# Batch 2's transposes issued earlier, both transposes of a pair ahead of their copies, score and value bursts merged

## The chip, the cores and the metric

The kernel runs on one core of one Trainium2 chip. The metric is the device time of one execution in microseconds (us); of several executions the median is given. The core's engines are TensorE (PE, matmuls), VectorE (DVE), ScalarE (ACT), GpSimd (POOL) and SyncE (SP). Each works through its own instructions in the order in which they stand; semaphores make one engine wait for another or for a DMA. SP and POOL also issue the DMAs.

## The reference

Eight batches, eight heads, 576 tokens, head dimension 64: attention in a window of 32 tokens to each side, with 8 global tokens that see all and are seen by all, and behind it a gated feed-forward layer on the 4608 tokens.

```python
scores = scale * np.matmul(q, k.transpose(0, 1, 3, 2))
mask = np.abs(pos[:, None] - pos[None, :]) <= window
mask = mask | is_global[:, None] | is_global[None, :]
scores = np.where(mask, scores, -1000000000.0)
...
attn = attn / (np.sum(attn, axis=-1, keepdims=True) + 1e-09)
attn_out = np.matmul(attn, v)
x = attn_out.transpose(0, 2, 1, 3).reshape(B * S, H * D)
silu = g * (1.0 / (1.0 + np.exp(-g)))        # g = x @ w_gate
out = silu * (x @ w_val) @ w_out
```

## The kernel before, in words

The feed-forward layer is the backbone. `ffn` (L647) works on 9 chunks of 512 tokens, and each chunk has 16 units: 12 gates and 4 outputs. A gate (`gate`, L650) makes 128 columns of both projections, pg and pv, with four matmuls each into two PSUM tiles of the pool `pf` (four buffers); ACT makes a tanh of pg (L663), DVE two products (gv L665, h L669). An output (`outp`, L673) makes 128 tokens of the result with 12 matmuls, ACT scales it to osb (L681, three buffers), and SP stores it (L683). The units are numbered through, and the number is called a slot.

The attention of a batch is cut into steps, which are put into gaps behind the units, so that PE has dense work around them:

- `step_T` (batches 0 and 1): PE transposes k and q of a pair of heads into PSUM; ACT copies kT (L346), DVE copies qT (L351). From batch 2 on kT and qT come by DMA: `cast_qk` (L105) has POOL write k and q as bf16 to DRAM (kf, qf), and `transpose_qk` (L113) has SP issue two transposing DMAs (L115, L119).
- `step_GT` transposes the gathered global keys and queries to gT; `step_S2` (L389) and `step_SG` (L371) are the scores of the global tokens, each a burst of 8 matmuls, an exponential on ACT and a mask product on DVE (p2, pg).
- `step_P2T` transposes p2, `step_AV2` (L420) makes the global tokens' values, and three DVE steps turn them into gvt.
- `step_S(u)`, u from 0 to 4 (L450): scores in the window, 16 matmuls, exponential (L458), band product on DVE (pt, L463).
- `step_AV(tp)`, tp from 0 to 3, and `step_AV8`: values from pg, gvt, pt, va and vb (L494, L503), then a normalisation on DVE (a reduction, a reciprocal, a product xa, L475 to L481). va is v by tokens in blocks of 128; vb is the same shifted by half a block, made from va by two DMAs that SP issues (`load_vb`, L123).
- `step_X(tp)` and `step_X8`: xa is transposed to xT, the feed-forward layer's input: by PE and a copy on ACT (L541, L547) for batches 0 to 2, by a DMA that SP issues for batches 3 to 7 (from XB = 3).

PSUM has three pools: `pf` with four buffers of one bank, `psc` and `pm` with one buffer of two banks each. Window scores, S2 and SG go to `psc`, most others to `pm`.

Batch 0 runs ahead of the first unit (the head). Batch 1 lies in the gaps of slots 0 to 17, one or two steps each; batch 2 starts at slot 19 with one gap a slot, and the later batches follow with a step every 1.08 or 1.1 slots (`STEP`, L55). `later` (L574) in batch b issues the transposes of batch b + 2, the gather of its global tokens and the cast of batch b + 3; `later_v` loads its v. Batch 1's `later` stands in gap 15 and asks for batch 3; the transposes of batch 2 are put at the front of gap 16:

```python
gaps[8].append(lambda: kqms.__setitem__(2, gather_mask(*gather(2))))
gaps[10].append(lambda: cast_qk(3))
for i, g in enumerate(last):
    gaps[16 + i] = g
gaps[16].insert(0, lambda: transpose_qk(2))
```

## Time and profile before

| | us |
|---|---|
| three executions | 394.91, 395.31, 396.77 |
| median | 395.31 |
| the profiled execution | 395.97 |
| its span, first to last instruction | 394.3 |
| PE busy in the span | 357.5 (91%) |
| DVE busy | 236.7 (60%) |
| ACT busy | 148.4 (38%) |
| POOL busy | 99.0 (25%) |
| mean granted clock of PE, of 1 | 0.961 |

The profile is of one execution. Its page gives the busy time of each engine, the same in 40 equal slices, the granted clock of PE, the chain of work that ended last, and groups of instructions with count, busy time, mean duration and the idle time ahead of them. Other views are the waits (who waited for whom), the timeline of an engine, windows (busy times in given stretches) and the chain of waits in order of time. A busy PE is not a PE at its peak, as matmuls are pipelined.

### The profile page before, as it was taken

The page shows a single profiled execution, that of the slowest core. Times are in us where ns is not written, and L with a number is a line of the kernel's source. Part 1 is how long each engine was busy: PE and PEld are TensorE (multiplying, and loading weights), DVE is VectorE, ACT ScalarE, POOL GpSimd, SP SyncE. Part 2 cuts the span into 40 slices and gives each one's busy share as a digit, 9 for nine tenths or more (in the row PEclk, how much of TensorE's full clock was granted, in tenths as well). Part 3 has the DMA queues.
Part 4 walks back from the last instruction along what each step waited for, and adds up shares of the span by engine and source line. Part 5 has one row for each costly group of instructions (what it writes and reads, how often), then busy time and mean ns, then how long its engine had stood idle before and what let it go on. Part 6 is the DMA issues. An engine that isn't in the chain of part 4 may idle for free.

```text
span 394.3 us, 7717 instructions
## 1 busy us (share of the span) xinstructions
PE 357.5 (91%) x3159; PEld 170.7 (43%) x3159; DVE 236.7 (60%) x467; ACT 148.4 (38%) x228; POOL 99.0 (25%) x114
## 2 busy tenths in 40 slices
PE   2458889992799999999999999999999999999995
PEld 2344444540254544444444444444444444444442
DVE  5645678352275388638963895489448935743750
ACT  2523445340253345234533533354235423323321
POOL 8836661746051143114412201100000000000000
PEclk9958999997589999999999999999999999999999
DMA  8999999999999799999989728952260121002002
GB/s 116 113 207 204 186 204 129 132 218 160 177 73 129 137 163 129 87 154 187 126 93 229 111 25 82 205 111 16 80 130 18 28 80 62 0 27 82 0 26 81
DMA packets 151987, 44.51 MB, mean 113 GB/s; under 512 B 138384, under 2 KB 146064, under 8 KB 151952
## 3 DMA queue, kind: packets, MB, share of 16 engines
q0 software_dynamic: 101472, 19.40, 59.9%
q1 hardware_dynamic: 50480, 24.63, 28.9%
q8 instruction: 24, 0.39, 0.4%
q14 instruction: 11, 0.09, 0.1%
HBM read 38.28 MB, written 16.52 MB: 139 GB/s over the span
## 4 chain that ended last, share of the span: by engine, by line
PE 82%; DMA 8%; DVE 3%; SPq 2%; ACT 2%; POOL 2%; issue 1%; DVEq 0%; POOLq 0%; ACTq 0%
PE pg L657 24%; PE po L676 24%; PE pv L657 22%; DMA qT<-qf 3%; PE ps_av L494 3%; PE ps_s L450 3%; PE ps_av L503 2%; DMA vb<-va 2%; DMA kg<-in_k_dram,gofs 1%; SPq L115 1%; DMA va<-in_v_dram 1%; PE ps_x L541 1%; PE ps_t L340 1%; PE ps_sg L371 1%; DVE h L669 1%
## 5 line engine op out<-in xcount | busy, mean ns | idle before, releaser
L657 PE MATMUL pg<-xT,wg_sb 128*128 128x512 bf16 x432 | 113.3, 385 | 1.4 <-ACT xT L547 1.4
L657 PE MATMUL pv<-xT,wv_sb 128*128 128x512 bf16 x432 | 112.6, 384 | 0.0
L663 ACT ACTIVATE th<-pg 128x512 bf16<-128x512 f32 x108 | 64.5, 597 | 92.2 <-PE pg L657 79.2
L665 DVE SCALAR_TENSOR_TENSOR gv<-th,pg 128x512 bf16<-128x512 bf16 x108 | 74.0, 685 | 41.8 <-ACT th L663 41.8
L676 PE MATMUL po<-wo_sb,h 128*128 128x512 bf16 x432 | 98.3, 380 | 0.0
L669 DVE TENSOR_TENSOR h<-gv,pv 128x512 bf16<-128x512 bf16 x108 | 74.3, 688 | 11.8 <-PE pv L657 0.8
L657 PEld LDWEIGHTS <-wv_sb 128*128 128x128 bf16 x432 | 42.7, 99 | 52.2 <-issue 2.2
L101 POOL DMA_DIRECT2D va<-in_v_dram x40 | 36.1, 1061 | 95.7 <-PE ps_av L503 82.1
L676 PEld LDWEIGHTS <-h 128*128 128x128 bf16 x432 | 40.1, 98 | 45.9
L657 PEld LDWEIGHTS <-wg_sb 128*128 128x128 bf16 x432 | 36.7, 98 | 41.8 <-issue 6.9
L681 ACT ACTIVATE osb<-po 128x512 f32<-128x512 f32 x36 | 21.5, 597 | 84.1 <-PE po L676 78.1
L463 DVE TENSOR_TENSOR pt<-pe,band 128x1024 bf16<-128x1024 bf16 (+1 forms) x40 | 25.6, 640 | 32.2 <-ACT pe L458 31.5
L458 ACT ACTIVATE pe<-ps_s 128x1024 bf16<-128x1024 f32 (+1 forms) x40 | 37.5, 939 | 17.0 <-PE ps_s L450 16.3
L475 DVE TENSOR_REDUCE den<-ps_av 128x8 f32<-128x16 f32 (+1 forms) x40 | 6.8, 170 | 35.7 <-PE ps_av L503 29.9
L481 DVE TENSOR_TENSOR xa<-ps_av,den 128x512 bf16<-128x512 f32 (+1 forms) x40 | 25.5, 638 | 1.6 <-DVE den L480 0.2
L494 PE MATMUL ps_av<-gvt,pg 128*64 128x264 bf16 x128 | 18.7, 303 | 2.1 <-DVE gvt L435 2.0
L503 PE MATMUL ps_av<-vb,pt 128*64 128x66 bf16 x256 | 18.3, 201 | 1.4 <-DMA vb<-va 1.4
L450 PE MATMUL ps_s<-qT,kT 64*128 64x64 bf16 x576 | 16.5, 197 | 3.0 <-ACT pe L458 1.6
L450 PEld LDWEIGHTS <-kT 64*128 64x128 bf16 x576 | 11.9, 98 | 17.0 <-issue 15.8
L503 PEld LDWEIGHTS <-pt 128*64 128x64 bf16 x512 | 18.3, 117 | 1.9 <-DMA vb<-va 1.7
L503 PE MATMUL ps_av<-va,pt 128*64 128x66 bf16 x256 | 18.5, 201 | 0.0
L108 POOL DMA_DIRECT2D qf<-in_q_dram x6 | 16.6, 2766 | 0.0
(92 smaller groups left out, 187.9 us busy)
## 6 DMA issues: line engine op xcount, KB each, us to landing
out_dram<-osb SPq DMA_DIRECT2D x36, 256.0 KB, 2.2
vb<-va SPq DMA_DIRECT2D x16, 264.0 KB, 7.6
kf<-in_k_dram POOLq DMA_DIRECT2D x6, 576.0 KB, 8.4
qf<-in_q_dram POOLq DMA_DIRECT2D x6, 576.0 KB, 14.0
va<-in_v_dram POOLq DMA_DIRECT2D x24, 128.0 KB, 3.9
va<-in_v_dram POOLq DMA_DIRECT2D x16, 96.0 KB, 12.7
wg_sb<-in_moe_w_gate_dram POOLq DMA_DIRECT2D x3, 512.0 KB, 10.4
wv_sb<-in_moe_w_val_dram POOLq DMA_DIRECT2D x3, 512.0 KB, 13.1
```

What stands on the lines that cost most here:

```text
L101: nc.gpsimd.dma_start(out=va[lo:hi, u, :, 0:D], in_=vs[t0 + lo : t0 + hi])
L450: nc.tensor.matmul(out=ps[:, par, 64 * slot : 64 * slot + 64], lhsT=kT[r : r + 64, hp, 64 * t : 64 * t + P], rhs=qTs[b][r : r + 64, hp, 64 ...
L458: nc.scalar.activation(out=pe, in_=ps[:, :, 0 : 64 * ns].rearrange("p r (s c) -> p r s c", c=64), func=AF.Exp, scale=SCALE,)
L463: nc.vector.tensor_tensor(out=pt.rearrange("p r s c -> p (r s) c"), in0=pe.rearrange("p r s c -> p (r s) c"), in1=bc(band, [[0, 2 * ns], [ ...
L481: nc.vector.tensor_tensor(out=xa.rearrange("p (g h) d -> p g h d", g=g), in0=bc(ps, pst + [[1, D]]), in1=bc(den, [[4, g], [1, 4], [0, D]]) ...
L494: nc.tensor.matmul(out=ps[64 * e : 64 * e + 64, hg], lhsT=st["pg"][:, P * tp + 64 * e : P * tp + 64 * e + 64], rhs=st["gv"].rearrange("p h ...
L503: nc.tensor.matmul(out=ps[64 * e : 64 * e + 64, hg, hl, :], lhsT=pt[:, hl % 2, 4 * (hl // 2) + 2 * (tp % 2) + e, :], rhs=(va if e == 0 els ...
L657: nc.tensor.matmul(out=ps[:, 0:n], lhsT=w[:, cc, P * fc : P * (fc + 1)], rhs=xT[:, cc, t0 : t0 + n], start=(cc == 0), stop=(cc == NCC - 1),)
L663: nc.scalar.activation(out=th[:, 0:n], in_=pg[:, 0:n], func=AF.Tanh, scale=0.5)
L665: nc.vector.scalar_tensor_tensor(out=gv[:, 0:n], in0=th[:, 0:n], scalar=1.0, in1=pg[:, 0:n], op0=ALU.add, op1=ALU.mult,)
L669: nc.vector.tensor_tensor(out=st["h"][:, fc, 0:n], in0=gv[:, 0:n], in1=pv[:, 0:n], op=ALU.mult)
L676: nc.tensor.matmul(out=po, lhsT=st["h"][:, fc, P * ts : P * (ts + 1)], rhs=wo_sb[:, fc, :], start=(fc == 0), stop=(fc == NFC - 1),)
```

## The change

- `load_vb` for batch 0 copies on DVE; the other batches keep the DMAs.
- `step_T` issues the 24 transposes of k and q, then both copies.
- `step_SG` uses `pm`; AV of batch 2 from tp = 1 on uses `psc`, and AV8 from batch 3 on.
- The head has GT ahead of the second table step, vb and P2T ahead of S(1), and AV2 ahead of S(3).
- S2 with SG, S(1) with AV2, S(3) with AV(0) and others share a gap. Batches 1 and 2 have the same list `mid`; batches 3 to 7 have 10 entries, 1.6 slots apart, in place of 14.
- The first two gates of chunk 0 are split by tokens: `first_gates` does 384 columns of both ahead of X(3) of batch 0 and 128 behind it. Units 0 and 1 are then empty, and batch 1's T steps start one slot later.
- The transposes of batch 2 move from the front of gap 16 to the end of gap 14.

```diff
@@ load_vb
+        if b == 0:
+            nc.vector.tensor_copy(out=vb[0:64], in_=va[64:128, 0:4])
+            nc.vector.tensor_copy(out=vb[64:128], in_=va[0:64, 1:5])
+            return vb
@@ step_T
-                if name == "k":
-                    nc.scalar.copy(
...
-                else:
-                    nc.vector.tensor_copy(
...
+            nc.scalar.copy(
+                out=kT[:, hp, WIN : WIN + S].rearrange("p (i j) -> p i j", j=LJ),
+                in_=pss[0].rearrange("p j i -> p i j"),
+            )
+            nc.vector.tensor_copy(
+                out=qTs[b][:, hp, :].rearrange("p (i j) -> p i j", j=LJ),
+                in_=pss[1].rearrange("p j i -> p i j"),
+            )
@@ step_SG
-            ps = psc.tile([P, 2, 512], FP32, tag="sc", name="ps_sg")
+            ps = pm.tile([P, 2, 512], FP32, tag="m", name="ps_sg")
@@ step_AV
-            pool, tag = (psc, "sc") if tp % 2 and b == 0 or tp and b == 1 else (pm, "m")
+            pool, tag = (psc, "sc") if tp % 2 and b == 0 or tp and b in (1, 2) else (pm, "m")
@@ step_AV8
+            if b >= XB:
+                full = psc.tile([P, 2, 512], FP32, tag="sc", name="ps_av8")
...
@@ step_X
+            if b == 0 and tp == 3:
+                ps = pm.tile([P, HP, P], BF16, tag="m", name="ps_x")
...
@@ the lists of steps
-                L(step_T, 2), L(step_T, 3), tables_b, L(step_GT), L(step_S2), L(step_SG),
-                L(step_S, 1), L(step_P2T), L(step_S, 3), vb, L(step_AV2),
+                L(step_T, 2), L(step_T, 3), L(step_GT), tables_b, L(step_S2), L(step_SG),
+                vb, L(step_P2T), L(step_S, 1), L(step_AV2), L(step_S, 3),
...
+        mid = [
+            [L(step_S2), L(step_SG)],
+            [L(step_P2T), L(step_S, 0)],
+            [L(step_S, 1), L(step_AV2)],
+            [L(step_S, 2)],
+            [L(step_S, 3), L(step_AV, 0)],
+            [L(step_X, 0), L(step_AV, 1)],
+            [L(step_X, 1), L(step_AV, 2)],
+            [L(step_X, 2), L(step_AV, 3)],
+            [L(step_X, 3), L(step_S, 4), later],
+        ]
+        end = [[L(step_AV8), later_v], [L(step_X8)]]
...
-                [L(step_GT)], [], [], [L(step_T, 0)], [L(step_T, 1)],
+                [L(step_GT)], [], [], [], [L(step_T, 0)], [L(step_T, 1)],
                 [L(step_T, 2), L(step_T, 3), vb],
...
+            ] + mid, end
         if b < XB:
...
+            return [[L(step_GT), vb]] + mid + end
         return [
             [L(step_GT), vb],
-            [L(step_S2)],
-            [L(step_SG)],
-            [L(step_P2T), L(step_S, 0)],
-            [L(step_S, 1)],
-            [L(step_AV2)],
+            [L(step_S2), L(step_SG)],
+            [L(step_S, 0), L(step_P2T)],
+            [],
+            [L(step_S, 1), L(step_AV2)],
             [L(step_S, 2)],
-            [L(step_AV, 0), L(step_X, 0)],
+            [L(step_S, 3), L(step_AV, 0), L(step_X, 0)],
             [L(step_AV, 1), L(step_X, 1)],
-            [L(step_S, 3)],
-            [L(step_AV, 2), L(step_X, 2)],
-            [L(step_S, 4), later],
-            [L(step_AV, 3), L(step_X, 3)],
-            [L(step_AV8), L(step_X8), later_v],
+            [L(step_S, 4), L(step_AV, 2), L(step_X, 2), later],
+            [L(step_AV, 3), L(step_AV8), L(step_X, 3), L(step_X8), later_v],
         ]
@@ ffn
+        def first_gates(k):
...
+            def part(lo, hi):
+                for fc in range(k):
+                    for ps, w in zip(pss[fc], (wg_sb, wv_sb)):
+                        for cc in range(NCC):
+                            nc.tensor.matmul(
+                                out=ps[:, lo:hi], lhsT=w[:, cc, P * fc : P * (fc + 1)],
+                                rhs=xT[:, cc, t0 + lo : t0 + hi],
...
+                    if hi == CH:
+                        gate_after(fc, *pss[fc])
+
+            return [L(part, 0, CH - P), L(part, CH - P, CH)]
@@ the order of the whole
-    for f in head:
+    for f in head[:-1]:
         f()
+    first_gates, units0 = ffn(0, CH)
+    early, late = first_gates(2)
+    early()
+    head[-1]()
+    late()
...
-        gaps[i] = g + gaps[i]
+        gaps[1 + i] = g + gaps[1 + i]
     gaps[8].append(lambda: kqms.__setitem__(2, gather_mask(*gather(2))))
     gaps[10].append(lambda: cast_qk(3))
+    gaps[14].append(lambda: transpose_qk(2))
...
-    gaps[16].insert(0, lambda: transpose_qk(2))
...
-            at += STEP[b]
+            at += 1.0 if b < XB else 16.0 / len(steps)
```

More of the change, by code (lines that the diff above doesn't have):

```diff
@@ L512, in step_AV8 @@
             pt = st["p", 4]
[L513 removed]
+            if b >= XB:
+                full = psc.tile([P, 2, 512], FP32, tag="sc", name="ps_av8")
+                ps = full[:, 0, 0 : 4 * W].rearrange("p (h c) -> p h c", c=W)
+            else:
+                ps = mtile([P, 4, W], FP32, "ps_av8")
             for hg in range(2):
@@ L538, in step_X @@
                 return
-            ps = mtile([P, HP, P], BF16, "ps_x")
+            if b == 0 and tp == 3:
+                ps = pm.tile([P, HP, P], BF16, tag="m", name="ps_x")
+            else:
+                ps = mtile([P, HP, P], BF16, "ps_x")
             for hp in range(HP):
@@ L683, in outp @@
             nc.sync.dma_start(out=out[r0 : r0 + P, :], in_=osb)
-        L = lambda f, *a: (lambda: f(*a))
-        return [(n / CH * 1.73, L(gate, fc)) for fc in range(NFC)] + [
-            (2.6, L(outp, ts)) for ts in range(n // P)
-        ]
+        units = [L(gate, fc) for fc in range(NFC)] + [L(outp, ts) for ts in range(4)]
+        return units if t0 else (first_gates, units)
     head, s4, av8, x8 = attention(0)
-    for f in head:
+    for f in head[:-1]:
         f()
+    first_gates, units0 = ffn(0, CH)
[3 more added lines that the diff above has]
+    late()
     first, last = attention(1)
@@ L711 @@
                 assert slot < 16 * b - (b >= XB), (b, slot)
-            at += STEP[b]
+            at += 1.0 if b < XB else 16.0 / len(steps)
     n = 0
     for c in range(NT // CH):
-        for f in ffn(c * CH, CH):
-            f[1]()
+        units = ffn(c * CH, CH) if c else [lambda: None, lambda: None] + units0[2:]
+        for f in units:
+            f()
             for g in gaps.get(n, []):
```

56 lines of the change are left out of this document (17 added, 39 removed).

## The prediction

> **What bounds the kernel now.** I read the page first, for the busy share of TensorE (PE) and its granted clock in 40 slices of 9.9 us.
>
> ```profile
> PE   2458889992799999999999999999999999999995
> PEclk9958999997589999999999999999999999999999
> ```
>
> PE is full from slice 13 to the end; what it loses lies in the first three slices, in slices 4 to 6 and around slice 10, and the clock is down in two of these places. So I asked what ended PE's waits.
>
> ```profile
> PE ps_s L389 <- DMA kT<-kf: 7.9, 1, 7.9
> PE ps_t L340 <- ACT kT L346: 2.9, 4, 0.7
> PE ps_sg L371 <- DMA qT<-qf: 2.8, 1, 2.8
> ```
>
> The columns are the total, the count and the longest. The two greatest are one event: batch 2's global scores need kT and qT, which come by DMA. The timeline of SP's queue (start, duration of the issue) and of PE around it:
>
> ```profile
> 80.47 0.33 SPq L683 DMA_DIRECT2D out_dram<-osb  x1
> 80.92 3.53 SPq L115 DMA_TRANSPOSE kT<-kf  x1
> 84.56 2.67 SPq L119 DMA_TRANSPOSE qT<-qf  x1
> 87.32 5.40 SPq L115 DMA_TRANSPOSE kT<-kf  x1
> 92.81 6.48 SPq L119 DMA_TRANSPOSE qT<-qf  x1
> 100.02 0.55 SPq L127 DMA_DIRECT2D vb<-va  x1
> ```
>
> ```profile
> 89.50 1.03 PE L657 MATMUL pv<-xT,wv_sb 128*128 128x512 bf16 x4
> 98.38 0.72 PE L389 MATMUL ps_s<-kT,gT 128*32 128x320 bf16 x8 [7.86 <-DMA kT<-kf]
> ```
>
> The first pair is batch 3's, the second batch 2's (SP's order below), although batch 2's is due first: PE stands at 90.52 (98.38 less 7.86). The other 90% of the span is dense PE work, where only fewer or cheaper matmuls help.
>
> **The change part by part.** (1) Batch 2's transposes. On SP, rows before (kf2 is batch 2's key, kf3 batch 3's; osb are the rows that are stored):
>
> ```order
> L683 DMA out_0_dram<-osb_1247 128x512
> L683 DMA out_0_dram<-osb_1295 128x512
> L115 DMA_TRANSPOSE kT1_98<-kf3_1072 128x4x576
> L119 DMA_TRANSPOSE qT_1318<-qf3_1074 128x4x576
> L115 DMA_TRANSPOSE kT0_97<-kf2_213 128x4x576
> L119 DMA_TRANSPOSE qT_1348<-qf2_215 128x4x576
> L126 DMA vb_1425<-va0_95 64x2112
> ```
>
> and the same place on SP after:
>
> ```order
> L702 DMA out_0_dram<-osb_1263 128x512
> L115 DMA_TRANSPOSE kT0_97<-kf2_213 128x4x576
> L119 DMA_TRANSPOSE qT_1299<-qf2_215 128x4x576
> L702 DMA out_0_dram<-osb_1314 128x512
> L115 DMA_TRANSPOSE kT1_98<-kf3_1088 128x4x576
> L119 DMA_TRANSPOSE qT_1337<-qf3_1090 128x4x576
> L130 DMA vb_1441<-va0_95 64x2112
> ```
>
> Batch 2's pair moves past batch 3's pair and past one store; it now follows the third store, whose rows ScalarE (ACT) gives here, and the one landing of a qT that the trace tells, after a start with the queue to itself, is in the row of that tile (least, median, most):
>
> ```profile
> 76.27 0.60 ACT L681 ACTIVATE osb<-po 128x512 f32<-128x512 f32 x1 [2.45 <-PE po L676]
> DMA to landing us min/median/max: 7.2/7.2/7.2
> 92.81 12.54 DMA qT<-qf
> ```
>
> The pair can start at 76.87 + 0.45 (80.92 - 80.47, from a store to the transpose behind it) = 77.3 on the clock of before. PE asks for kT 90.5 - 77.3 = 13.2 us later and for qT 13.6 us later; both ends move together whatever is gained ahead of them. A pair with the queue to itself lands (84.56 - 80.92) + 7.2 = 10.9 us after its start; the pair of batch 2 before, in company, took 92.81 + 12.54 - 87.32 = 18.0. So between hidden and 4.4 us late. The company this time is the cast of batch 3, whose first half (k) GpSimd issued here, with q behind it:
>
> ```profile
> 69.57 2.28 POOL L108 DMA_DIRECT2D kf<-in_k_dram  x1
> ```
>
> It goes out just ahead, so I take a value beyond the middle, 15.6: **2.0 us of wait left of 10.7**, gain 8.7. With the wait goes the slow clock behind it:
>
> ```profile
> 98.00:106.00 8.00, 4.85 (x24) 1.31 (x24) 1.87 (x3) 1.30 (x2) 0.84 (x1) 0.50 1.68 177
> 106.00:111.00 5.00, 5.00 (x35) 2.27 (x32) 1.83 (x3) 2.08 (x4) 0.00 (x0) 0.51 1.74 143
> 90.00:94.00 4.00, 0.52 (x3) 0.12 (x2) 1.54 (x3) 0.29 (x1) 3.70 (x5) 0.98 1.93 158
> ```
>
> PE's busy time stands after the length, the clock third from the end: 4.85 x 0.50 + 5.00 x 0.49 = 4.9 us lost to half clock. The third row says that the clock fell about 3.3 us after PE went idle at 90.52 (a mean of 0.98 over 4 us is 0.16 us at half), so a wait of 2 us should not lower it: **gain 4.9** (none if the wait lasts over 3.3).
>
> (2) vb of batch 2 is still behind both pairs and now one store more. Before, its second half was issued 19.1 us after the first transpose and took a further
>
> ```profile
> DMA to landing us min/median/max: 5.2/8.2/8.3
> ```
>
> so 27.3, now about 27.8 after the pair's start. PE reaches the first value burst at 13.2 plus 4 gates and the bursts between. The chain of waits prices these:
>
> ```profile
> 252.38 0.86 PE pv L657 x4
> 253.24 0.11 PE ps_g L360 x2
> 253.35 0.86 PE pg L657 x4
> 255.08 0.39 PE ps_s L389 x8
> 255.47 0.97 PE pg L657 x4
> 259.49 0.34 PE ps_s L450 x16
> ```
>
> 4 x 1.83 for the gates, 0.39 twice for the global scores, four bursts of 0.34, some 0.7 for the transposes and the global values, 2.0 of wait: 12.2, in all 25.4. So a new wait of some 2.4 us on vb; with both pairs in company more (first rival), with neither none. VectorE (DVE) is also late there by about 0.8 us: in three gates it gets
>
> ```profile
> L665 DVE SCALAR_TENSOR_TENSOR gv<-th,pg 128x512 bf16<-128x512 bf16 x108 | 74.0, 685 | 41.8 <-ACT th L663 41.8
> L669 DVE TENSOR_TENSOR h<-gv,pv 128x512 bf16<-128x512 bf16 x108 | 74.3, 688 | 11.8 <-PE pv L657 0.8
> L463 DVE TENSOR_TENSOR pt<-pe,band 128x1024 bf16<-128x1024 bf16 x32 | 22.2, 694 | 13.8 <-ACT pe L458 13.1
> L481 DVE TENSOR_TENSOR xa<-ps_av,den 128x512 bf16<-128x512 f32 x32 | 22.1, 692 | 1.3 <-DVE den L480 0.2
> ```
>
> three times 1.37 + 0.69 and twice a step of 0.69 with small ones around it, say 1.06 (gvt, then the normalisation that writes xa): 8.3 against PE's 7.5 (three gates, three bursts of 0.34, the global values and the first values). A wait on vb lets DVE catch up, so the two don't add: I take 2.0, near the 2.4 that the rows of before give. **Cost 2.0** for both, 0 to 8.
>
> (3) Both transposes of a pair ahead of their copies (batch 1): PE's four waits of 0.7 for the copy of kT fall. The next user of each of these PSUM tiles comes a gate (1.83, below) later; the copy on ACT is the wait of 0.7, that on DVE takes 0.75 (below), and both now run side by side under that gate. **Gain 2.8**; if a copy were still late, down to 0.
>
> (4) Merged bursts. In the rows just shown the gate after scores takes 0.97, after ps_g 0.86: 0.11 a return. PE's order goes from dense matmuls into scores or values 82 times before and 51 times after (S2 with SG, S with AV, S with AV2, AV3 with AV8). 31 x 0.11: **gain 3.4**, between 2 (should a change of kind within a burst cost as much as half of a return) and 4.5 (should S2 and SG overlap too).
>
> (5) The head. DVE's rows there, before (mg and mg2 are masks, gT feeds the global scores, gvt and pt the values):
>
> ```order
> L304 SCALAR_TENSOR_TENSOR mg2_218<-ps_i_378,thi_163,mt_119 128x640
> L308 TENSOR_SCALAR mg_217<-iq_133,sgn_161,thr_159 128x576
> L365 COPY gT_386<-ps_g_383 128x256
> L401 TENSOR_TENSOR p2_399<-p2e_397,mg2_218 128x640
> L383 TENSOR_TENSOR pg_412<-pge_410,mg_217 128x576
> L463 TENSOR_TENSOR pt_433<-pe_431,band_169 128x1024
> L463 TENSOR_TENSOR pt_462<-pe_460,band_169 128x1024
> L427 TENSOR_TENSOR gvt_488<-ps_av2_467,dmask_139 128x528
> ```
>
> and after:
>
> ```order
> L369 COPY gT_381<-ps_g_378 128x256
> L308 SCALAR_TENSOR_TENSOR mg2_218<-ps_i_383,thi_163,mt_119 128x640
> L312 TENSOR_SCALAR mg_217<-iq_133,sgn_161,thr_159 128x576
> L405 TENSOR_TENSOR p2_399<-p2e_397,mg2_218 128x640
> L387 TENSOR_TENSOR pg_412<-pge_410,mg_217 128x576
> L127 COPY vb_414<-va0_95 64x2112
> L128 COPY vb_414<-va0_95 64x2112
> L467 TENSOR_TENSOR pt_444<-pe_442,band_169 128x1024
> L431 TENSOR_TENSOR gvt_467<-ps_av2_446,dmask_139 128x528
> ```
>
> gT is ahead of the masks, two copies take vb's place on SP, and gvt has one product less ahead of it. From the chain of waits and the timelines of DVE and PE before:
>
> ```profile
> 18.21 8.33 DMA vb<-va
> 19.65 0.46 DVE L383 TENSOR_TENSOR pg<-pge,mg 128x576 bf16<-128x576 bf16 x1 [0.73 <-ACT pge L378]
> 23.09 0.69 DVE L463 TENSOR_TENSOR pt<-pe,band 128x1024 bf16<-128x1024 bf16 x1 [1.03 <-ACT pe L458]
> 24.75 0.43 PE L494 MATMUL ps_av<-gvt,pg 128*64 128x264 bf16 x2 [2.04 <-DVE gvt L435]
> 26.58 0.26 PE L503 MATMUL ps_av<-vb,pt 128*64 128x66 bf16 x1 [1.39 <-DMA vb<-va]
> ```
>
> va is there at 18.2, when vb's last DMA went out; pg, done at 20.1 before, comes up to 1.7 us earlier (my estimate) by gT's move and SG's own PSUM tile. Copies from about 18.5, each 2112 elements of bf16. No row shows such a copy: by the pt row (694 ns for 1024, two inputs, SBUF) it is at 0.6 ns an element some 1.27 us, by the copy from PSUM (754 ns for 576) some 2.8:
>
> ```profile
> L351 DVE COPY qT<-ps_t 128x576 bf16<-128x576 bf16 x8 | 6.0, 754 | 3.7 <-PE ps_t L340 3.7
> ```
>
> SBUF to SBUF is nearer to the first: done at 21.0, then from pt's start to the first values 1.66 as before (24.75 - 23.09), values from 22.7 and their first vb at 22.9. **Gain 3.7**; 0.6 with 2.8 a copy, 4.4 with copies so quick that the scores' own chain ends last. The Trainium skill ("VectorE: DVE Perf Modes", "The perf-mode tier table") gives 693 ns for a bf16 copy of 2048 elements in SBUF; by that, an estimate, the gain would be the 4.4 above and the time 0.7 lower; no row of before shows it.
>
> Against the copies: while DVE works, GpSimd issues weight loads, but then idles:
>
> ```profile
> 27.16 0.39 POOL L231 TENSOR_TENSOR kqm<-kg,mka 128x128 bf16<-128x128 f32 x1 [6.35 <-DMA kg<-in_k_dram,gofs]
> ```
>
> A delay of 1 or 2 us disappears in those 6.35. The Trainium skill ("SBUF — State Buffer", "Who interferes with whom") says that such a copy locks GpSimd out, descriptors included; that would delay these issues by the length of the copies, and the row above covers it.
>
> The early gates on 384 columns stand ahead of X3:
>
> ```profile
> 33.14 0.40 PE L541 MATMUL ps_x<-ident,xa 128*128 128x128 bf16 x4 [0.73 <-DVE xa L481]
> 34.21 1.02 PE L657 MATMUL pg<-xT,wg_sb 128*128 128x512 bf16 x4 [0.67 <-ACT xT L547]
> ```
>
> They fill the first wait, but they themselves wait for X2's copy, like the second row's 0.67, and the late gates for X3's: 1.34 in place of 1.40, so 0. If the clock (5 in slice 3) rises late, their 16 matmuls of three quarters of 0.86 / 4 cost twice their 2.6: up to 2.6 lost.
>
> **Sum.** 8.7 + 4.9 - 2.0 + 2.8 + 3.4 + 3.7 = 21.5 us. The profiled execution took 395.97 (span 394.3), 0.66 over the median of 395.31; 374.5 in its terms, **373.8** as a median. About 0.5% (2 us) is what a measurement of this kernel can tell from none.
>
> **Rivals.** (A) Both pairs travel in company, as batch 2's did. qT is 4.4 late (2.4 more), past the 3.3 us at which the clock falls (4.9 more); SP then spends 12.0 on each pair's issue (99.29 - 87.32), so vb lands near 34 while PE wants it near 27.7, 4 more than I took: 385. For: the cast ahead; against: batch 3's pair needed 10.9. (B) Both pairs travel as batch 3's did: nothing waits for qT or vb (4.0 less) and the copies of the head cost next to nothing (4.4 in place of 3.7): 369. (C) The pair doesn't start earlier because something else holds SP, kf2 or qf2 landing late: parts 3 to 5 alone, 9.9 us, 385; against it, the cast of batch 2 stands far ahead of batch 3's on GpSimd's queue. (D) Slower: DVE paces the merged value bursts of batches 3 to 7. If each of three value bursts waits for a product and a normalisation (1.76), 5.3 a batch and 26 in all: 400. It decides from 21.5 / 5 = 4.3 us a batch. In the five gates around these bursts the two are about even (five times 1.37, three products and three normalisations on DVE, five times 1.83 and 2.8 of bursts on PE: each near 12); against it, four output units without DVE work follow in each chunk, and PE's buffers bridge two gates, so I expect less than 1 us a batch.
>
> **How the numbers follow.** Forecast 0.60, A 0.10, B 0.20, C 0.04, D 0.04, and 0.02 that gains and costs end within 0.5%. All but D and the last are faster by over 0.5%: 0.94, within 0.02, slower 0.04. The range, 368 to 382, holds the forecast with its open costs (vb to 8, slow copies, late clock, DVE up to 1 a batch) and B; A, C, D and the rest, 0.20, lie outside.
>
> **What would show it.** Right: kT and qT of batch 2 issued behind the third store, PE's wait for them under 3 us and no second stretch at half clock; no wait of ps_t for ACT; the first values with vb some 4 us earlier than 26.58; vb waits, if any, in batch 2 alone. Wrong: half clock again near 85 us, PE waits on DVE in every chunk, vb copies over 2 us each.

## The result and the profile after

The changed kernel takes 384.62 us (median; 383.31 to 385.63) where the kernel before takes 395.76: ratio 0.972, 95% interval 0.968 to 0.976. The gain is 11.1 us, not the 21.5 of the forecast, and the time lies outside its range. Executions of one kernel differ here by up to 12 us (and one each of the kernel before, e7 and f4 took 720, 597 and 460, unexplained), so a ratio compares only executions within 1.5% of the fastest of their kernel, and the table of the experiments gives the median and the least of all beside it. The profiled execution took 384.5 (span 382.8). The page's row of PE and of its clock, 40 slices of 9.6 us:

```profile
PE   2678999979899679988999999999999999999995
PEclk9999999999999969999999999999999999999999
```

The head is fuller, and the hole around slice 10 has shrunk to small dips; but there is a new one in slices 14 and 15, with the clock down in the second, where PE was full before. The waits of PE (total, count, longest):

```profile
PE ps_av L424 <- DMA p2t<-p: 7.3, 2, 6.0
PE ps_sg L375 <- DMA qT<-qf: 2.7, 1, 2.7
PE ps_av L507 <- DMA vb<-va: 1.5, 1, 1.5
```

The 7.9 for kT and the four waits of ps_t are gone, 2.7 for qT is left, and p2t, which made nobody wait long before, heads the list. Where the time came and went is read from ScalarE's copies of the fourth store of each chunk (start, duration): before, chunks 0 to 2,

```profile
79.85 0.60 ACT L681 ACTIVATE osb<-po 128x512 f32<-128x512 f32 x1 [2.50 <-issue]
135.37 0.60 ACT L681 ACTIVATE osb<-po 128x512 f32<-128x512 f32 x1 [1.62 <-issue]
173.92 0.60 ACT L681 ACTIVATE osb<-po 128x512 f32<-128x512 f32 x1 [1.88 <-issue]
```

and after:

```profile
72.65 0.60 ACT L700 ACTIVATE osb<-po 128x512 f32<-128x512 f32 x1 [2.50 <-issue]
118.49 0.60 ACT L700 ACTIVATE osb<-po 128x512 f32<-128x512 f32 x1 [1.89 <-issue]
167.13 0.60 ACT L700 ACTIVATE osb<-po 128x512 f32<-128x512 f32 x1 [5.50 <-PE pg L650]
```

Chunk 0 lasts 72.7 us in place of 79.9 and chunk 1 45.8 in place of 55.5: 16.9 gained. Chunk 2 lasts 48.6 in place of 38.6: 10.1 given back. The later chunks together gain 4.5. In chunk 2 stands this chain (start, duration, what), of the view of the work that ended last:

```profile
125.87 0.26 DVE pt L467
126.12 10.27 DMA p2t<-p
136.39 0.04 issue
136.44 0.74 PE ps_av L424 x19
```

p2t is batch 3's. Its source was written by VectorE early enough, but SP was busy, and GpSimd had just sent the two casts (k and q) of batch 5 and batch 4's v. VectorE, SP and GpSimd (start, duration of the issue):

```profile
121.44 0.48 DVE L405 TENSOR_TENSOR p<-p2e,mg 128x640 bf16<-128x640 bf16 x1
```

```profile
110.60 6.03 SPq L115 DMA_TRANSPOSE kT<-kf  x1
116.73 6.39 SPq L119 DMA_TRANSPOSE qT<-qf  x1
123.21 1.53 SPq L702 DMA_DIRECT2D out_dram<-osb  x3
124.92 0.47 SPq L130 DMA_DIRECT2D vb<-va  x1
125.48 0.55 SPq L131 DMA_DIRECT2D vb<-va  x1
126.12 1.28 SPq L410 DMA_TRANSPOSE p2t<-p  x1
```

```profile
107.31 2.28 POOL L108 DMA_DIRECT2D kf<-in_k_dram  x1
109.08 2.78 POOL L108 DMA_DIRECT2D qf<-in_q_dram  x1
110.78 5.27 POOL L101 DMA_DIRECT2D va<-in_v_dram  x5
```

p2t was ready to go at 121.9, went out at 126.1 behind batch 4's pair, three stores and vb, and took 10.3 to land (median 3.5 before). PE asked at 130.40 (136.44 less 6.04). Before, the same transfers of SP and GpSimd stood apart:

```profile
133.29 2.53 SPq L115 DMA_TRANSPOSE kT<-kf  x1
135.92 3.01 SPq L119 DMA_TRANSPOSE qT<-qf  x1
147.42 1.22 SPq L406 DMA_TRANSPOSE p2t<-p  x1
```

```profile
112.06 2.28 POOL L108 DMA_DIRECT2D kf<-in_k_dram  x1
```

The cast of batch 5 was 21 us ahead of batch 4's pair there, and the pair took 5.5 of SP, not 12.4. Behind the wait the clock fell (after; third from the end):

```profile
133.40:140.20 6.80, 3.55 (x27) 1.64 (x29) 1.51 (x4) 0.60 (x1) 2.46 (x3) 0.50 0.94 63
```

6.0 of wait and 6.8 x 0.5 = 3.4 of half clock: 9.4 of the 10.1. (The 1.2 that remain of the 7.3 are batch 4's p2t, in chunk 3.)

### The profile page after: what moved, and what is told of

It reads as the page before. It is cut to its first block, busy times and chain, and to the rows that moved or that the text cites. A ratio compares the mean times of both kernels' runs of the same rounds, so it can differ in the third digit from the quotient of the medians.

```text
span 382.8 us, 7690 instructions
## 1 busy us (share of the span) xinstructions
PE 346.2 (90%) x3125; PEld 173.5 (45%) x3175; DVE 235.3 (61%) x469; ACT 147.4 (39%) x228; POOL 99.8 (26%) x114
## 4 chain that ended last, share of the span: by engine, by line
PE 78%; DMA 11%; DVE 5%; issue 3%; ACT 2%; SPq 0%; POOL 0%; DVEq 0%; ACTq 0%; POOLq 0%
PE po L695 24%; PE pg L650 21%; PE pv L650 20%; DMA p2t<-p 5%; PE ps_av L498 3%; DMA qT<-qf 3%; PE ps_s L454 2%; PE ps_av L507 2%; DMA vb<-va 2%; DMA q_bf<-in_q_dram 1%; PE ps_t L346 1%; PE ps_x L552 1%; DVE h L688 1%; DVE gv L684 1%; ACT pe L462 1%
## 5 line engine op out<-in xcount | busy, mean ns | idle before, releaser
L650 PE MATMUL pv<-xT,wv_sb 128*128 128x512 bf16 x420 | 109.2, 381 | 1.9 <-ACT osb L700 1.4
L650 PE MATMUL pg<-xT,wg_sb 128*128 128x512 bf16 x393 | 106.9, 382 | 3.4 <-DVE gv L684 0.8
L695 PE MATMUL po<-wo_sb,h 128*128 128x512 bf16 x417 | 94.0, 379 | 2.1 <-issue 1.9
L688 DVE TENSOR_TENSOR h<-gv,pv 128x512 bf16<-128x512 bf16 x108 | 74.3, 688 | 11.7 <-PE ps_av L507 0.5
L650 PEld LDWEIGHTS <-wv_sb 128*128 128x128 bf16 x424 | 41.7, 98 | 52.4 <-issue 3.1
L700 ACT ACTIVATE osb<-po 128x512 f32<-128x512 f32 x36 | 21.5, 597 | 93.5 <-PE po L695 74.0
L650 PEld LDWEIGHTS <-wg_sb 128*128 128x128 bf16 x424 | 37.6, 98 | 43.8 <-issue 4.8
L101 POOL DMA_DIRECT2D va<-in_v_dram x40 | 37.1, 1195 | 63.8 <-PE ps_av L507 45.1
L467 DVE TENSOR_TENSOR pt<-pe,band 128x1024 bf16<-128x1024 bf16 (+1 forms) x40 | 25.4, 635 | 11.0 <-ACT pe L462 10.3
L454 PEld LDWEIGHTS <-kT 64*128 64x128 bf16 x576 | 11.5, 98 | 16.2 <-issue 15.4
L235 POOL TENSOR_TENSOR kqm<-kg,mka 128x128 bf16<-128x128 f32 x8 | 3.2, 395 | 54.6 <-DMA kg<-in_k_dram,gofs 54.6
## 6 DMA issues: line engine op xcount, KB each, us to landing
kf<-in_k_dram POOLq DMA_DIRECT2D x6, 576.0 KB, 10.3
```

Of the source, the lines that this page charges most:

```text
L101: nc.gpsimd.dma_start(out=va[lo:hi, u, :, 0:D], in_=vs[t0 + lo : t0 + hi])
L454: nc.tensor.matmul(out=ps[:, par, 64 * slot : 64 * slot + 64], lhsT=kT[r : r + 64, hp, 64 * t : 64 * t + P], rhs=qTs[b][r : r + 64, hp, 64 ...
L467: nc.vector.tensor_tensor(out=pt.rearrange("p r s c -> p (r s) c"), in0=pe.rearrange("p r s c -> p (r s) c"), in1=bc(band, [[0, 2 * ns], [ ...
L650: nc.tensor.matmul(out=ps[:, 0:n], lhsT=w[:, cc, P * fc : P * (fc + 1)], rhs=xT[:, cc, t0 : t0 + n], start=(cc == 0), stop=(cc == NCC - 1),)
L688: nc.vector.tensor_tensor(out=st["h"][:, fc, 0:n], in0=gv[:, 0:n], in1=pv[:, 0:n], op=ALU.mult)
L695: nc.tensor.matmul(out=po, lhsT=st["h"][:, fc, P * ts : P * (ts + 1)], rhs=wo_sb[:, fc, :], start=(fc == 0), stop=(fc == NFC - 1),)
```

## The experiments

The kernel before had medians of 397.4 to 397.8 beside these runs; the ratio is to that kernel, and e2 and g1 have none on record. Chunks are those of the profiled execution, worked out as above; its time stands beside them, since it is not always near the median.

| kernel | median (least) us | ratio, interval | profiled us | chunks 0, 1, 2, 3 |
|---|---|---|---|---|
| before | 395.8 (394.9) | | 396.0 | 79.9, 55.5, 38.6, 38.3 |
| changed | 384.6 (383.3) | 0.972, 0.968 to 0.976 | 384.5 | 72.7, 45.8, 48.6, 38.5 |
| e1 P2T of batch 3 on PE | 386.4 (384.5) | 0.970, 0.964 to 0.977 | 386.2 | 76.0, 48.5, 40.2, 42.8 |
| e2 pair 4 later | 382.7 (374.8) | | 374.8 | 73.2, 46.1, 39.5, 37.8 |
| e3 cast 5 later | 386.2 (384.8) | 0.968, 0.962 to 0.975 | 386.1 | 73.2, 50.8, 46.9, 36.7 |
| e4 no move | 396.8 (393.6) | 0.998, 0.996 to 1.001 | 393.6 | 72.8, 60.5, 39.4, 42.7 |
| e5 vb 2 on DVE | 388.2 (384.3) | 0.972, 0.966 to 0.977 | 387.5 | 73.4, 46.4, 47.8, 40.9 |
| e6 the same, pair 4 later | 382.0 (375.8) | 0.950, 0.945 to 0.956 | 383.7 | 76.1, 48.7, 39.7, 41.6 |
| e7 casts wait | 391.4 (384.6) | 0.974, 0.967 to 0.982 | 386.7 | 72.4, 46.5, 39.9, 44.0 |
| e8 vb 2 on DVE, P2T on PE | 382.7 (378.7) | 0.962, 0.956 to 0.967 | 378.7 | 73.2, 47.9, 39.9, 39.6 |
| e9 vb 2 early, pair 4 later | 385.6 (382.8) | 0.969, 0.966 to 0.973 | 388.8 | 76.1, 42.0, 47.9, 43.0 |
| e10 e9, plain first gates | 385.0 (378.8) | 0.957, 0.952 to 0.961 | 389.9 | 74.3, 43.4, 52.2, 38.5 |
| e11 before, lists merged | 414.3 (413.5) | 1.045, 1.041 to 1.048 | 413.5 | 81.1, 55.1, 37.9, 49.7 |
| e12 e9, old copies | 390.0 (387.1) | 0.979, 0.975 to 0.983 | 393.3 | 75.7, 42.7, 56.4, 39.6 |
| f1 no casts 4 to 7 | 378.3 (376.3) | 0.952, 0.947 to 0.957 | 380.7 | 74.4, 50.6, 39.7, 37.8 |
| f2 batch 3 from gap 34 | 382.3 (378.6) | 0.961, 0.956 to 0.966 | 383.9 | 71.9, 50.5, 36.9, 43.8 |
| f3 the same, vb 2 early | 379.5 (373.4) | 0.957, 0.952 to 0.962 | 373.4 | 72.6, 42.8, 36.4, 40.5 |
| f4 p2t on ACT's queue | 390.8 (385.3) | 0.980, 0.973 to 0.987 | 391.1 | 75.3, 48.8, 46.1, 42.4 |
| g1 vb 2 early, P2T on PE | 383.9 (377.0) | | 387.1 | 73.6, 47.6, 47.6, 40.2 |
| g2 before, move alone | 393.1 (386.6) | 0.977, 0.970 to 0.985 | 394.2 | 81.5, 50.1, 38.6, 40.0 |

The first theory was that p2t of batch 3, by its place on SP, is the whole loss (Q); its rival, that the parts gave less than their terms and PE would wait for something else anyway (S).

**e1: P2T of batch 3 off SP**

```diff
         def step_P2T():
-            if b >= XB:
+            if b > XB:
```

> Batch 3's P2T by TensorE and ScalarE (as batch 2's) in place of a DMA on SP. Theory Q (the missing gain is batch 3's p2t, which stands on SP behind batch 4's pair of transposes: 6.0 us of wait and about 3.4 us of half clock behind it): both go, five transposes of some 0.5 us and a return of 0.11 come, 384.6 - 9.4 + 0.6 = 375.8, and no clock below 1 after 100 us. Rival S (the parts simply gave less than their terms, and the wait only stands where PE would otherwise wait for DVE or vb): the wait moves to the next tile of batch 3, 382 to 385.

Its chunk 2 is 8.5 us shorter, as Q said, but the kernel is not faster: chunk 1 is 2.6 longer (vb of batch 2 was 5.6 late), chunk 3 4.3 longer (batch 4's p2t 2.6 late, half clock behind it), and chunk 0 3.4 (2.5 of it the early gates, below). Q alone falls.

**e2: batch 4's pair behind batch 3's P2T**

```diff
         def later():
             if b + 2 < B:
-                transpose_qk(b + 2)
+                if b != 2:
+                    transpose_qk(b + 2)
...
+    gaps[35].append(lambda: transpose_qk(4))
```

> Batch 4's pair of transposes issued three gaps after batch 3 has issued its P2T, not before it. Theory Q: p2t goes out as soon as p2 is there, lands within 4 us, no wait and no half clock: 384.6 - 9.4 = 375.2. Rival S: 382 to 385. Rival K (the pair is needed where it is: batch 4's kT or qT come late in its place): a wait for kT or qT near 155 us, 378 or more.

One execution, the profiled one, took 374.75, with no wait for vb or batch 3's p2t (2.3 for qT was its longest for a batch): 21.2 us under the 395.97 of the profiled kernel before, where the forecast said 21.5. The others took 379.6, 385.8 and 386.4, so in two of four the remedy gained nothing.

**e3: cast of batch 5 and v of batch 4 later**

```diff
-            if b + 3 < B:
+            if b + 3 < B and b != 2:
                 cast_qk(b + 3)
...
+    gaps[35] += [lambda: cast_qk(5), lambda: load_v(4)]
```

> The cast of batch 5 and batch 4's v issued seven gaps later, so that batch 4's pair travels without company, in its old place on SP. Theory Q with company as the reason for the long issue: the pair takes some 6.2 us of SP (3.5 and 2.7) and not 12.4, p2t goes out when p2 is there: 375.2. If the pair is slow by itself (Q without company), SP is still held until about 123: 384.

The edit moved nothing: no other instruction stands between these places on GpSimd, whose queue runs ahead, so the cast went out at 110.74. The kernel is the changed one over again, and so its profile is worth having. PE's wait in chunk 1, and its row of p2t:

```profile
100.91 0.26 PE L507 MATMUL ps_av<-vb,pt 128*64 128x66 bf16 x1 [6.00 <-DMA vb<-va]
```

```profile
PE ps_av L424 <- DMA p2t<-p: 4.6, 1, 4.6
```

The same program waits 6.0 for batch 2's vb here and 1.5 in the other profile, 4.6 and 6.0 for p2t, with half clock behind each long wait, and takes 386.2. So there are at least two places. From here the theory was (W, later B): PE has become early against the DMAs; whichever transfer lands last makes it wait.

**e4 and g2: part 1 undone, and part 1 alone**

```diff
-    gaps[14].append(lambda: transpose_qk(2))
...
+    gaps[16].insert(0, lambda: transpose_qk(2))
```

> The changed kernel with batch 2's transposes back behind batch 3's (part 1 undone). If part 1 gave what the prediction took for it (8.7 of wait and 4.9 of clock, less 2.0), 384.6 + 11.6 = 396, with a wait of some 10 us for kT and qT near 88 us and a half clock behind it. If a good part of the gain came from elsewhere, 388 to 392.

> The kernel before with part 1 alone: batch 2's pair behind the third store, nothing else changed; batch 2 keeps its 16 gaps, so the DMAs keep their time. The prediction's part 1 and 2: 11.6 less than before, ratio 0.971, with batch 3's p2t on time (3.5 us to landing before). If the move alone brings the late p2t of batch 3 too: ratio 0.985 or more.

Without the move the rest of the change is worth nothing (0.998): PE came earlier and waited 10.0 for kT and 5.9 for qT, in place of 7.9 and 2.8. But batch 3's p2t was on time in e4 (chunk 2 39.4): part of what undoing the move cost in chunk 1 was won back there. The move alone, put into the kernel before, gives 4.7 in the median (9.0 by its ratio, from two of the six executions) where 11.6 were expected: vb of batch 2, behind batch 3's pair, which took 14.4 from 88.36 on beside batch 4's cast (out at 85.88), was 8.6 late with half clock behind it, and chunk 1 50.1. This is the second half of the prediction's rival A. Batch 3's p2t was on time (chunk 2 38.6).

**e5, e6, e8: batch 2's vb by VectorE**, alone, with e2's and with e1's edit

```diff
-        if b == 0:
+        if b in (0, 2):
             nc.vector.tensor_copy(out=vb[0:64], in_=va[64:128, 0:4])
```

> Batch 2's vb by two copies on VectorE, as batch 0's, in place of two DMAs on SP; batch 3's p2t still stands behind batch 4's pair. All numbers on the scale on which the changed kernel takes 384.6. Theory W (two transfers on SP stand behind a pair of transposes that travels in the company of a cast: batch 2's vb, whose wait is 1.5 in one execution and 6.0 in another, and batch 3's p2t, 4.6 to 6.0, each with some 3.4 of half clock where it is long): the first goes, the second stays, 380 to 383, with a p2t wait near 130 us in the profile. Rival S (the parts gave less than their terms; the waits only take up slack): 384 to 386.

> Batch 2's vb by copies on VectorE and batch 4's pair issued after batch 3's P2T. Theory W: neither wait is left; 374 to 376 in nearly every execution, no half clock after 95 us. Rival S: 382 to 385. Rival K (something later in the queue takes the wait over, as batch 2's vb took over from batch 3's p2t): 378 to 382 with a wait over 3 us in another place.

> Batch 2's vb by copies on VectorE, batch 3's P2T by TensorE and ScalarE; batch 4's pair where the change puts it. Theory W: 375 to 377 (0.6 of transposes more than the other remedy), unless batch 3's vb, which still stands behind the pair, comes late too. Rival S: 382 to 385.

e5 shows the p2t wait that was to stay (4.8) and gains nothing: 388.2, over both of its expectations. e6 and e8 have chunks 2 of 39.7 and 39.9 without it; in the median they are 15.7 and 15.0 us under the kernel before, the changed kernel 11.1, so W's two places hold some 4 of the missing 10 in most executions and all of it in few; both medians are well over the 374 to 377 of theory W. In e6's profile P2T of batch 2 waited 3.9 for VectorE (last section).

**e7, f1, f4: order or load**

```diff
-            t = dram.tile([S, H, D], BF16, name=f"{name}f{b}")
+            t = flat[name, b - 1] if b > 3 else dram.tile([S, H, D], BF16, name=f"{name}f{b}")
```

> Casts of batches 4 to 7 written into the DRAM tile of the batch before, so that a cast can't start before the pair of that batch has been read; all orders as in the changed kernel. Theory W with company as the cause: batch 4's pair takes some 6.2 us of SP (3.5 and 2.7, the pair of batch 3 before) and not 12.4, batch 2's vb lands without a cast beside it, 375 to 378. If pairs are as slow without a cast (transposes slow each other, or stores do), 384 or more, since the casts now also land later.

```diff
-                cast_qk(b + 3)
+                no_cast(b + 3)
```

> The changed kernel without the casts of batches 4 to 7 (their pairs read batch 2's and so compute other scores; all else, and every order, as in the changed kernel). Theory B (the DMA engines: cast, pair, v and small transfers of a batch share them, and whatever lands last makes PE wait, so what PE gains ahead of them comes back as a wait in one place or another): with a large part of that work gone, no wait over 1.5 us for p2t, vb or osb after 95 us, 371 to 376, and the executions lie within 3 us of each other. Rival S (the parts gave less than their terms): 380 or more, with less waiting than in the changed kernel but more of something else.

```diff
-                nc.sync.dma_start_transpose(out=st["p2t"], in_=st["p2"])
+                nc.scalar.dma_start_transpose(out=st["p2t"], in_=st["p2"])
```

> The changed kernel with the P2T transposes of batches 3 to 7 issued from ScalarE's DMA queue and not from SP's. Theory Q (SP's order: p2t waits until the pair, three stores and vb have been issued): p2t goes out 4 us earlier, lands in 3 to 4 us, no wait, 375 to 377. Theory B (the DMA engines themselves): it goes out earlier but lands as late, beside the pair and the cast, wait 3 to 6 us, 382 to 386.

In f1 SP's order is the changed kernel's, and its rows are:

```profile
117.17 2.78 SPq L119 DMA_TRANSPOSE kT<-kf  x1
120.00 4.18 SPq L123 DMA_TRANSPOSE qT<-qf  x1
124.27 1.75 SPq L706 DMA_DIRECT2D out_dram<-osb  x3
```

The pair takes 7.0 and not 12.4, and from chunk 2 on PE waits for no DMA longer than 0.5. So the load makes the pair slow, not the place (batch 4's v still travels in f1, spread from 103.5 to 120.7). In e7 the pair took even 5.4, but the casts, now behind the pairs, met the p2t that follow: batch 3's took 10.2 to land, batch 4's 11.9, batch 5's 8.6, and chunks 3 and 4 paid (44.0 and 43.6). The Trainium skill ("DMA: Bandwidth & Descriptors", "Queues, rings and completion order") says that each DMA engine takes turns between the queues that have work, packet by packet; the 12.4 with a cast beside and 7.0 without agree. f1 still has batch 2's vb 5.6 late, with no cast of batch 4 about; what slowed it is not settled, and so f1 missed its own 371 to 376. f4 can't decide: on ScalarE's queue the transpose, ready at 127.5, went out at 133.9, when SP's pair and stores had gone out (the profile names a store as releaser), and ScalarE stood still for 4.6 us.

**f2, f3: more time for the DMAs**

```diff
         steps = attention(b)
+        if b == 3:
+            at = 34.0
...
-    gaps[14].append(lambda: transpose_qk(2))
+    gaps[14] += [lambda: transpose_qk(2), lambda: vbs.__setitem__(2, load_vb(2))]
```

> Batch 3 begins at gap 34 and not 31 (it began at 35 before), with its 16 gaps and those of the later batches behind it: the DMAs get three gaps, 5.7 us, more between batch 4's pair and batch 3's P2T. Theory B: p2t of batch 3 is no longer late in most executions (6.0 and 3.4 of half clock less), 376 to 380, the rest being vb of batch 2 where it is late; batch 4's p2t as before. Rival S: 383 to 386.

> Batch 3 from gap 34, and batch 2's vb right behind batch 2's pair. Theory B: batch 2 gains 3 to 4 us as with vb moved alone (chunk 1: 42.0 to 43.4 us), and 5.7 us more for the DMAs behind it: 372 to 377. If the time won in batch 2 is asked back at once by the DMAs of batches 3 and 4 (as with vb moved alone, where 6.7 to 11 us of wait for a full osb came instead): 380 to 386.

The first hunk is f2, both are f3. With batch 3 three gaps later p2t is on time (chunk 2: 36.9 and 36.4, where some of batch 3's work has moved on to chunk 3; the two together take 80.7 and 76.8, and 87.1 in the changed kernel). The price is in chunk 3: its first gate waits 3.6 us in f2, with half clock behind it, and 3.0 in f3, until 162.89 in f2. The profile names no releaser; batch 3's xT transpose went out at 158.44, and those four take 4.4 to land. f3 has the lowest median of the versions that compute everything: 379.5 against the changed kernel's 384.6, ratio to the kernel before 0.957, its best execution 373.4 with a granted clock of 1.0 throughout. By the ratio e6 (0.950) can't be told from it, as the intervals overlap. Neither f2 nor f3 reached what theory B said (376 to 380, 372 to 377).

**e9, g1: SP's order alone, and the version meant as best**

> SP's order alone: batch 2's two vb DMAs right behind batch 2's pair (ahead of batch 3's), batch 4's pair behind batch 3's P2T. On the scale on which the changed kernel takes 384.6. Theory W: neither vb of batch 2 nor p2t of batch 3 is late; 374 to 378, chunks 1 and 2 of the stores some 46 and 39.5 us long (45.8 and 48.6 in the changed kernel's profile, 50.8 and 46.9 in that of its equal, the cast experiment). Rival S: 382 to 385. Rival K: batch 4's p2t takes a wait over with half clock, chunk 3 some 42 and not 37.8, 379 to 382.

> A version meant to be faster than both: the changed kernel with batch 2's vb right behind batch 2's pair and the P2T of batches 3 and 4 by TensorE, so that neither stands behind a pair of transposes. Theory B, by the shortest stretch that each chunk showed so far with such an edit (73 for chunk 0, 42.5, 40, 38, 38, then 35.2, 37.2, 31.1 and 31.1, and 5.7 to the end): 372 where nothing else is late, median 374 to 378, since the early gates at half clock (2.5) and stores behind batch 5's pair can still come. If the DMAs ask all of it back: 382 to 386.

e9 is e2's edit with f3's second hunk; g1 that hunk with P2T of batches 3 and 4 on PE (`if b > XB + 1`). In the profiled execution, e9's slowest of six, chunk 1 is the shortest of all (42.0), and chunk 2 asks it all back: batch 5's pair travels with the cast of batch 6 (out at 139.65), takes 13.8 of SP, and the stores of chunk 2 stand behind it, so ScalarE has no osb to write and PE no PSUM.

```profile
148.41 6.24 SPq L115 DMA_TRANSPOSE kT<-kf  x1
154.75 7.43 SPq L119 DMA_TRANSPOSE qT<-qf  x1
162.27 1.01 SPq L704 DMA_DIRECT2D out_dram<-osb  x2
```

```profile
166.66 1.86 PE L652 MATMUL pv<-xT,wv_sb 128*128 128x512 bf16 x4 [6.75 <-ACT osb L702]
```

g1's profile had the same wait (7.3), and its median, 383.9, is what it said for DMAs that ask all of it back; e9's, 385.6, is over all that it said. That is rival K of these runs, in e9 at batch 4's p2t too, where K had put it (2.4 late, half clock behind it, chunk 3 43.0): a remedy in one place is paid for in the next.

**e10, e12: two terms of the sum**, both on e9

```diff
-    early, late = first_gates(2)
-    early()
     head[-1]()
-    late()
+    for f in units0[0:2]:
+        f()
```

> As the run before, with the first two gates whole and behind X3, as in the kernel before. If the early gates bring nothing and cost 2.5 us where the clock rises late (1.28 us for each group of four in two profiles, 0.65 in seven), the best executions stay within 0.5 us of the run before and the worst get 2 to 3 us shorter. If they do fill the wait for ACT, all get 1 to 1.5 us longer.

> As the first run of this job, with the copy of kT ahead of the transposes of q again. The prediction's part 3 says 2.8 us more, all of it in chunk 0 (four waits of 0.7 of ps_t for ACT back). If the waits only move, nothing.

In both e9's and e10's profile the clock rose late; with early gates that makes chunk 0 76.1, without them 74.3, and e2's, with early gates at full clock, is 73.2. So they cost 1.8 in the one case; the other wasn't met without them. The whole times decide nothing here: e10's best is 3.9 under e9's and its worst 1.4 over, which neither expectation said, and the wait for a full osb alone was 11.2 in its profile. e12 has its four waits back, and its chunk 0 is 2.5 longer than e2's, both with the early gates at full clock:

```profile
PE ps_t L347 <- ACT kT L353: 2.9, 4, 0.7
```

**e11: the merged lists alone, in the kernel before**

```diff
         return [
             [L(step_GT), vb],
-            [L(step_S2)],
-            [L(step_SG)],
-            [L(step_P2T), L(step_S, 0)],
+            [L(step_S2), L(step_SG)],
+            [L(step_S, 0), L(step_P2T)],
...
-            at += STEP[b]
+            at += STEP[b] if b < XB else 1.4
```

> The kernel before, with the merged lists of batches 3 to 7 alone (five entries less a batch; SG in its own PSUM tile, AV8 in that of the scores). By the prediction's 0.11 an entry: 25 x 0.11 = 2.8 us less than before, ratio 0.993. If merging saves more than the returns (chunks 3 to 6 together are 4.5 us shorter in the changed kernel than in the one before): 4.5 to 6, ratio 0.985 to 0.989. If DVE paces the merged bursts: slower.

17.0 slower. To have batch 3 ready I put ten entries 1.4 gaps apart, 14 gaps a batch where the kernel before has 15.1 to 15.4. This is no clean test of merging, then, but one of the DMAs' time: PE waited for p2t in three batches,

```profile
PE ps_av L421 <- DMA p2t<-p: 10.3, 3, 7.1
```

with half clock, and chunks 3 and 4 took 49.7 and 46.6 for 38.3 and 38.9.

## Why the prediction was wrong

**The step that failed** is (2), at the place where it ends: the sum put every wait for a transfer behind batch 2's vb at nothing, and gave no reason ("vb waits, if any, in batch 2 alone"). I followed SP's queue from batch 2's pair to batch 2's vb and stopped. The change moves batch 4's pair 22.7 us forward with PE (133.29 to 110.60), as it also shortens batch 2 from 16 entries to 12, but the cast of batch 5 only 4.8 (112.06 to 107.31), as GpSimd's queue runs ahead of PE. So the pair, which took 5.5 before, now travels with the cast and takes 12.4 of SP, as the forecast itself had worked out for such company in rival A (12.0), and batch 3's p2t stands behind it. No term of the sum stood for this. The lists bring the two closer as well: the pair stands at gap 28 and the P2T at 34, six gaps, 11 us, apart; before they stood eight apart (30 and 38), and 14 us in the trace, p2t landing in 3.5. That alone did no harm: in e4, which has the changed lists, they are 11.3 apart too (125.50 and 136.77), but the cast went out 16 ahead of the pair (109.27), the pair took 4.9, p2t landed in 5.1, and nobody waited for it. In the profiled execution the p2t wait and its half clock are 9.4 of the 10.8 that were missing, and 1.2 are batch 4's p2t.

**What the runs show in its place** is wider than that one row. In the 20 traces batch 4's pair takes 5.0 to 7.3 us, from start to end, in the seven in which it goes out ahead of a cast, after the cast has landed, or without one (before, e4, e7, e11, f1, f3, g2); 11.9 to 16.1 in the twelve in which it goes out with a cast on its way; and 9.3 in e2, where the next cast follows it. Ahead of batch 3 the change gained 16.9 us; the DMAs that feed batches 2 to 5 were not made any faster. Each remedy shortened the chunk it was for (chunk 2 from 48.6 to between 36.4 and 40.2 in e1, e2, e6, e8, f1, f2, f3; chunk 1 to 42.0 in e9), and in most executions another transfer was late elsewhere. The medians say how much was left: 11.1 us under the kernel before for the change, 11.3 and 11.7 in e1 and e9, 15 to 16 in e2, e6, e8 and f2, 18.0 with more time and an earlier vb (f3), 19.3 with less load (f1). The ratios agree but for e6: 0.972, 0.970 and 0.969, then 0.950, 0.962 and 0.961 (e6, e8, f2), 0.957 and 0.952. So less load gives back 8.2 of the missing 10.8, a remedy for batch 3's p2t alone 0.2 (e1) or 3.9 (e2). That DMA load is what PE runs into is shown for batch 4's pair and batch 3's p2t; for batch 2's vb it is not, and why one execution loses at vb and the next at p2t stays open.

The other steps, one by one. (1) was right: kT and qT went out behind the third store, the pair landed 16.3 after its start (70.14 to 86.41; 15.6 taken), 2.7 of wait were left (2.0 forecast), and there was no half clock in chunk 1 of this profile (with the same move, e2, e5, e7, e8 and f2 have 3.4 or 6.8 us of it from 86 or 87 on). That e4, without the move, costs 10.6 beside e3, against the 11.6 of (1) and (2), is luck: by the profiles its chunk 1 is 14.7 longer than the changed kernel's, its chunk 3 4.2 longer, and its chunk 2 9.2 shorter. And the clock's threshold of 3.3 us did not hold (below). (2) in itself: vb landed 27.8 after the pair's start in this profile, as forecast, 1.5 late; but 29.0 to 32.5 in e1, e3, f1 and f2, up to 6.0 late with half clock; the range of 0 to 8 was the honest part. (3) was right: 2.9. (4) was too small. Over all matmul starts of chunks 4 to 6 before, dense to dense takes 0.22 and dense to small 0.31, small to small 0.02 and small to dense 0.14: 0.09 going in and 0.11 coming back, and I had priced the return alone. Those three chunks have 18 entries less (43 and 25) and are 4.7 shorter, but a batch's opening steps have moved out of them; over chunks 2 to 6, with 29 entries less, the change gains 5.0 when the 10.6 of p2t and its half clock are left out (29 x 0.20 = 5.8). (5) was right, at its upper end: copies of 704 ns, and the first value matmul with vb at 22.09, 4.5 ahead of 26.58.

```profile
L127 DVE COPY vb<-va x1: 704/704/704, 18.4 to 18.4; 64x2112 bf16<-64x2112 bf16 x1
```

```profile
22.09 0.26 PE L507 MATMUL ps_av<-vb,pt 128*64 128x66 bf16 x1
```

The Trainium skill's figure there ("VectorE: DVE Perf Modes", "The perf-mode tier table"), 693 ns for 2048 elements, agrees with it. The early gates came out as the bound said: nothing, or 2.5 lost where the clock rose late. The first two groups of e1 and of the changed kernel start 1.24 and 0.65 apart (the clock rows read 1.00 there in both; the trace's first record of full clock comes at 33.98 in e1 and at 27.55 in the changed kernel):

```profile
29.17 1.44 PE L669 MATMUL pg<-xT,wg_sb 128*128 128x384 bf16 x4 [0.67 <-ACT xT L558]
30.41 1.49 PE L669 MATMUL pv<-xT,wv_sb 128*128 128x384 bf16 x4
```

```profile
28.48 0.81 PE L669 MATMUL pg<-xT,wg_sb 128*128 128x384 bf16 x4 [0.67 <-ACT xT L558]
29.13 0.81 PE L669 MATMUL pv<-xT,wv_sb 128*128 128x384 bf16 x4
```

Of the rivals, A's time (385) came out for a different cause, which is luck: in this profile batch 2's qT was only 2.7 late. A's late vb is what e3, e1 and g2 show. C's 385 is luck too, as the pair did start earlier; and B, where nothing waits for qT or vb, was not met in this profile. D did not happen: PE's waits for gvt and gv come to 1.0 and 0.8 in the whole span.

## What to carry to other kernels

When a change makes the fast engine earlier, follow every queue that feeds the stages behind it, up to the first transfer that still has slack, and count the distance in time between a long transfer and the short one behind it before and after. Look also at what else will be on its way then: a queue that does not wait for the fast engine stays where it was, and what was apart before may travel together. Merging or shortening a stage takes time from the transfers of the next one; a gain of 17 us came back as 10 of waiting one chunk later. And where several transfers run with little slack, one profile shows only one of the ways in which they fall out.

## What the hardware showed that I had not expected

**The clock falls after waits much shorter than 3.3 us, and not always.** In the changed kernel PE waited 2.74 for qT and kept its clock; in e7 it waited 1.99 at the same place and lost it (PE's rows and windows of the changed kernel, then of e7; clock third from the end):

```profile
86.45 0.43 PE L375 MATMUL ps_sg<-qT,gT 128*32 128x288 bf16 x8 [2.74 <-DMA qT<-qf]
...
86.00:90.00 4.00, 3.50 (x40) 1.86 (x42) 1.84 (x3) 2.22 (x4) 4.00 (x4) 1.00 1.18 222
```

```profile
85.48 0.43 PE L375 MATMUL ps_sg<-qT,gT 128*32 128x288 bf16 x8 [1.99 <-DMA qT<-qf]
...
85.00:89.00 4.00, 3.52 (x27) 1.67 (x29) 1.70 (x3) 1.26 (x3) 0.41 (x2) 0.74 1.25 223
89.00:93.00 4.00, 3.94 (x62) 2.04 (x62) 2.17 (x4) 3.06 (x4) 2.51 (x2) 0.83 1.06 243
```

4 x 0.26 + 4 x 0.17 = 1.7 us lost. The Trainium skill ("TensorE: Matmul & The Clock Gate", "HAM oscillation — how this bites in real kernels") gives the rule "no PE-idle gaps >~3.4µs"; here the measurement decides, and gaps of 2.0 (e7), 2.3 (e2) and 2.6 (e5) were enough.

The clock records of the traces say more. In all 20 the clock changes only at points 3.41 us apart, which lie elsewhere in each execution; half clock lasts 3.41, 6.83, 10.2, 13.7 or 17.1 us. Between two such points at full clock, 1.97 us or more of PE's idle time (all gaps added up, by the modelled ends of the matmuls) were followed by half clock in all 34 cases; the longest idle time that was not is 1.96 (f3), and the shortest that was is 1.43 (g2). The changed kernel's wait fell across a point, 85.58, with 1.93 idle ahead of it; e7's lay between two, 83.52 and 86.93, with 1.96.

**A copy on VectorE was held up while GpSimd issued DMAs.** In e6 the second copy of vb took 4.55 us in place of 0.70. VectorE and GpSimd:

```profile
86.43 0.70 DVE L127 COPY vb<-va 64x2112 bf16<-64x2112 bf16 x1
87.17 4.55 DVE L128 COPY vb<-va 64x2112 bf16<-64x2112 bf16 x1
```

```profile
86.37 2.56 POOL L108 DMA_DIRECT2D kf<-in_k_dram  x1
88.46 2.72 POOL L108 DMA_DIRECT2D qf<-in_q_dram  x1
```

It ended at 91.7, when the issue of the second cast (to 91.2) had ended. The first copy had run beside the first cast's issue in its usual 0.70. My prediction had only the other direction. The Trainium skill ("SBUF — State Buffer", "Who interferes with whom") says that whoever issues first has the shared ports for the whole instruction and the other blocks; one event is no proof, but it agrees. In e5, where both copies were done before the cast was issued, they took 0.70 each.
